# Final stage of an FFT convolution and phase-mixing kernel: the transpose of u by a transposing DMA in place of TensorE

## The chip, the cores and the metric

The kernel runs on one core of one Trainium2 chip. The metric is the device time of one execution, in microseconds (us). Three runs of the kernel before gave 2108.34, 2110.66 and 2111.68 us; the median is 2110.66 us.

## What is computed

Two layers follow one another on `x` of 8 batches x 5696 tokens x 128 channels. The first is a long convolution along the tokens, done by FFT. The second mixes tokens with two 5696 x 5696 matrices, and ends with a small product per token:

```
y  = irfft(rfft(x, 2S) * rfft(h, 2S))[:S]          # first layer, its output is x of the second
theta  = x @ w_theta
zr, zi = x * cos(theta), x * sin(theta)
y  = w_tok_r @ zr + w_tok_i @ zi                    # over tokens, for each batch and channel
u  = x + y
out = u + max(u @ w_ch, 0)                          # the final stage: w_ch is 128 x 128
```

The final stage needs `u @ w_ch`. TensorE sums over partitions, and `u` comes with tokens on partitions, so `u` is transposed to channels on partitions before the product.

## The kernel before

**The order of the stages.** The FFT layer fills about the first 510 us. Then comes the mixing, in two passes over the columns of the token matrices (the sum over source tokens, split in two halves of 2816 tokens, and a remainder of 64). Pass 0 (`p == 0`) sums over the first half and stores partial sums in HBM (`cp_hbm`). Pass 1 (`p == 1`, from about 1285 us) loads those partial sums back, adds the second half and the remainder, and runs the final stage. The change lies in pass 1, save for one moved call in pass 0.

**Pairs and stretches.** Rows of output are worked on in pairs: token tile `tt` and token tile `22 + tt`, each of 128 tokens, and each in two halves of 512 columns (4 batches x 128 channels). So a pair has four output blocks of 128 x 512. The kernel uses Strassen's scheme of seven products (M1 to M7) for a pair, in the order M3, M4, M5, M2, M1, M7, M6 (loop index `n` = 0 to 6). The sum over source tokens is cut in four *stretches* (groups of 3, 3, 3 and 2 blocks of 256), so in one stretch the loop at L1079 issues seven *blocks* of 6 matmuls (4 in the last stretch, and one more for the remainder in four of its blocks). Some pairs at the start of a pass (tt 0, and tt 1 in pass 0) use the plain product ("classic", L1034), and the last 64 tokens have stretches of their own (L953).

**What feeds TensorE.** The weights are loaded by GpSimd's DMA queue (L509) into a ring of six buffers, each by four DMAs of 80 or 96 KB. VectorE transposes them (L714, `wt`) and forms the sums that the scheme needs (L723, `out_`); it also adds the finished products to the output blocks (L1091, two additions for most products, in the last stretch of a pair). At the start of pass 1 the z operands `b` come through ScalarE's DMA queue (L639).

**The output blocks.** In pass 1 a block `c` is loaded by SyncE's queue from `cp_hbm` (L828) into one of six buffers, is added to, goes through the final stage, and is stored to `out` by the same queue (L805). The four blocks of a pair are c12, c21, c11, c22; they go through the final stage one after the other, one in each stretch of the *next* pair, and the load of the fourth block of a pair (c22) goes into the buffer of the second block of the pair before (c21), so it waits for that block's store.

**The final stage, `u_stage` (L785).** `first` makes a bf16 copy `ub` of the block on ScalarE (L791), transposes it by four TensorE transposes of 128 x 128 into the PSUM tile `utp` (L794), and copies that to SBUF as `uts` on ScalarE (L796). `uts` is one buffer, `yt_room()`, a piece of the ring tile, so it is free again only when the product of the block before has read it. `second` issues four matmuls with `w_ch` into `v` (L801), `max(v, 0) + c` on VectorE (L803), and the store (L805). Both PSUM tiles use the bank tagged `misc`.

**Where they are called.** `aside(first_of, second_of)` (L940) is called after each block: where `first_of` is true it takes the next `first` from the list `spread`, where `second_of` is true it runs the pending `second`. In the Strassen loop it is `aside(n == 1, n == 4)` (L1108), in the classic one `aside(n == 0, n == 2)` (L1055). In pass 0 the same calls place background steps of the phase computation (`bg_phase`: transposes L742, theta matmuls L396, ScalarE's and VectorE's steps L398 to L432). The last four blocks of the kernel call `first` and `second` themselves at L1094 to L1104, with tags of their own for `utp`, `v` and `uts`.

Of 90 output blocks, 86 go through `spread`: 4 in the stretches of the last 64 tokens at the start of pass 1, 2 (of 64 tokens) in the pair after them, and 80 in the 20 pairs that follow.

The order of instructions is made by a scheduler from the program's order and the dependencies; VectorE's order is written out by hand only up to the first Strassen pair of a pass.

Of the kernel before, what the change touches and what calls it, by code (L numbers as in the profile page):

```python
# [11 lines left out]
BF16 = mybir.dt.bfloat16  # L12
# [10 lines left out]
def kernel(  # L23
# [10 lines left out]
    nc = tc.nc  # L34
    B, S, D = x.shape
    assert D == 128
    P = 128
# [454 lines left out]
    def small(at, n):  # L492
        return ring["all"][:, WB + BT + at:WB + BT + at + n]
# [5 lines left out]
    def yt_room():  # L499
        return small(0, 4 * P).rearrange("p (b n) -> p b n", b=4)  # L500
# [101 lines left out]
    for g, (bp, dh) in enumerate(groups):  # L602
        st = {}
# [59 lines left out]
    def sum_some(n):  # L663

        for o in [o for o in owed if o[1] <= 2 or done["used"] > o[0]][:n]:
            owed.remove(o)
            o[2]()
# [117 lines left out]
    def u_stage(ti, h, c, m):  # L785
        st = {}

        def first(tags=("misc", "misc", None)):
            st["tags"] = tags
            ub = ybp.tile([P, 4, D], BF16, tag="yb", name="ub")  # L790
            nc.scalar.activation(ub[:m].rearrange("p b d -> p (b d)"), c[:m], AF.Copy)  # L791
            utp = mps.tile([P, 4, P], BF16, tag=tags[0], name="utp")
            for b in range(4):
                nc.tensor.transpose(utp[:, b, :m], ub[:m, b, :], ident_bf[:m, :m])  # L794
            st["uts"] = uts = cp.tile([P, 4, P], BF16, tag=tags[2], name="uts") if tags[2] else yt_room()
            nc.scalar.activation(uts[:, :, :m], utp[:, :, :m], AF.Copy)  # L796

        def second():
            v = mps.tile([P, 512], F32, tag=st["tags"][1], name="v")
            for b in range(4):  # L800
                nc.tensor.matmul(v[:m, b * D:(b + 1) * D], st["uts"][:, b, :m], w_ch_sb,  # L801
                                 start=True, stop=True)
            nc.vector.scalar_tensor_tensor(c[:m], v[:m], 0.0, c[:m],  # L803
                                           op0=ALU.max, op1=ALU.add)
            nc.sync.dma_start(  # L805
                bass.AP(tensor=out.tensor, offset=out.offset + ti * P * D + 4 * h * S * D,
                        ap=[[D, m], [S * D, 4], [1, D]]),
                c[:m].rearrange("p (b d) -> p b d", b=4))
        return nothing, first, second

    tags, where_bg = {"n": 0}, {}
# [100 lines left out]
    nxt, second, st = None, None, {}  # L912
    ordered = ExitStack()
    for i, (k, p, tt, j0, s0, nj) in enumerate(stretches):
# [25 lines left out]
        def aside(first_of, second_of):  # L940
            nonlocal second
            if first_of and spread and (p == 1 or (tt > 0 and not end_of_pair)):
                where_bg["tags"] = ("c2", "c3") if j0 + s0 == TJ else ("red", "mag")
                _, first, second = spread.pop(0)
                with tc.issue_after(sides["late"].ins) if p == 0 and tt == 1 else ExitStack():
                    first()
                    if len(spread) > 1:
                        spread[1][0]()
            if second_of and second is not None:
                second()  # L950
                second = None

        if tt is None:  # L953
# [7 lines left out]
            for j in range(nj):  # L961
                jj = j0 + s0 + j
                for r in range(2):
                    b = [x[:, r, :] for x in bts[jj]]
# [37 lines left out]
        def product(a, jj, j, n, hs):  # L1002
            for r in range(2):
                for h in hs:
                    nc.tensor.matmul(ms[n // 2 * 2 + h], a[n][:, j, :, r],  # L1005
                                     bts_of[p][jj][n % 2 * 2 + h][:, r, :],
                                     start=(n % 2 == 0 and jj == 0 and r == 0), stop=False)
# [26 lines left out]
        if classic:  # L1034
            for n in range(4):
                for j in range(nj):
                    product(a, j0 + s0 + j, j, n, range(2))
                    if p == 0 and (n * nj + j) % 4 != 3:
                        sum_some(1)
                if end_of_pair and n % 2:  # L1040
                    (c12, z12), (c21, z21), (c11, z11), (c22, z22) = cs
                    out_of = (((c11, z11, 0), (c12, z12, 1)), ((c21, z21, 2), (c22, z22, 3)))[n // 2]
                    for h, (c, z, m_) in enumerate(out_of):
                        if p:
                            nc.tensor.matmul(ms[m_], wl[n // 2], zl[h], start=False, stop=True)
                            nc.vector.tensor_tensor(c, z, ms[m_], op=add)
                            continue
                        if n == 1:
                            nc.tensor.matmul(ms[m_], ident_bf, z, start=False, stop=True)
                        else:  # L1050
                            for b in range(4):
                                nc.tensor.matmul(ms[m_][:, b * D:(b + 1) * D], z[:, b, :], ident_bf,
                                                 start=False, stop=(b == 3))
                        nc.scalar.activation(c, ms[m_], AF.Copy)
                aside(n == 0, n == 2)  # L1055
            if end_of_pair and woven:
                for n_ in range(7):
                    step(n_)
            for j in range(nj):
                if p == 0:  # L1060
                    done["used"] = tt * (j0 + s0 + nj)
                else:
                    for op in sum_ops(bts[j0 + s0 + j])[:2]:
                        op()
        else:
            left = {}
            if zl is not None and end_of_pair:
                left = {M5: (wl[0], zl[1]), M7: (wl[0], zl[2]),
                        M2: (wl[1], zl[0]), M6: (wl[1], zl[2])}
            if end_of_pair:  # L1070
                (c12, z12), (c21, z21), (c11, z11), (c22, z22) = cs
                sums = {M3: ((c12, z12, add), (c22, z22, add)), M4: ((c11, z11, add), (c21, z21, add)),
                        M5: ((c11, c11, ALU.subtract), (c12, c12, add)),
                        M2: ((c21, c21, add), (c22, c22, ALU.subtract)),
                        M1: ((c11, c11, add), (c22, c22, add)),
                        M7: ((c11, c11, add),), M6: ((c22, c22, add),)}
            while owed and owed[0][0] < j0 + s0 + nj:
                sum_some(1)
            for n, q in enumerate(ORDER):  # L1079
                sum_some(1)  # L1080
                for j in range(nj):
                    jj = j0 + s0 + j
                    for r in range(2):
                        nc.tensor.matmul(ms[q], a[q][:, j, :, r], bts[jj][q][:, r, :],  # L1084
                                         start=(jj == 0 and r == 0),
                                         stop=(jj == NJ - 1 and r == 1 and q not in left))
                if q in left:
                    nc.tensor.matmul(ms[q], left[q][0], left[q][1], start=False, stop=True)  # L1088
                if end_of_pair:
                    for c, z, op in (sums[q][::-1] if i + 1 == len(stretches) and q == M5 else sums[q]):  # L1090
                        nc.vector.tensor_tensor(c, z, ms[q], op=op)  # L1091
                    if i + 1 == len(stretches):
                        if n == 4:
                            ends = [u_stage(t, h, c, P) for (t, h), (c, _) in zip(where, cs)]  # L1094
                            ends[0][1]((f"m{M3}", f"m{M5}", "yy0"))
                        elif n == 5:
                            ends[1][1]((f"m{M4}", f"m{M2}", "yy1"))
                        elif n == 6:
                            ends[0][2]()
                            ends[2][1]((f"m{M1}", f"m{M3}", "yy2"))  # L1100
                            ends[1][2]()
                            ends[3][1]((f"m{M7}", f"m{M5}", "yy3"))
                            ends[2][2]()
                            ends[3][2]()  # L1104
                    if woven:
                        for n_ in {1: (0, 1), 2: (2,), 3: (3,), 4: (4,), 5: (5,), 6: (6,)}.get(n, ()):
                            step(n_)
                aside(n == 1, n == 4)  # L1108
        if not end_of_pair:
            continue  # L1110
        if i + 1 == len(stretches):
# [35 lines left out]
```

## Time and profile before

| | |
|---|---|
| median of three runs | 2110.66 us (2108.34 to 2111.68) |
| the profiled execution, first to last instruction | span 2116.2 us |
| TensorE busy | 2008.1 us, 95% of the span |
| VectorE busy | 1598.3 us, 76% |
| ScalarE busy | 673.9 us, 32% |
| utp transposes, L794 | x360, busy 34.6 us |
| `uts` copies of the 86 blocks, L796 | x86, busy 50.9 us |
| `ub` copies, L791 | x90, busy 56.3 us |
| v matmuls of the 86 blocks, L801 | x344, busy 33.5 us |
| DMA, all queues | 334.97 MB, 408265 packets |

The profile is one execution. Of it only the span is given, no separate total; it is 5.5 us (0.26%) longer than the median of the timed runs. Engines are PE (TensorE's matmuls), PEld (its weight loads), DVE (VectorE), ACT (ScalarE), POOL (GpSimd) and SP (SyncE); a q behind a name is the engine's queue, which issues DMAs and waits. Matmuls overlap: a group of short ones ends later than the next one starts, so what they take of TensorE is read from the distance between starts. L794 stands for line 794 of the kernel. "A wt<-ring" after an engine means that the instruction writes `wt` and reads `ring`.

### The profile page before, as it was taken

The numbers are of one execution on the slowest core, as the hardware profiler recorded it, in microseconds if no ns is written. First come the engines' busy times: TensorE is split into PE (matmuls) and PEld (weight loads), VectorE is DVE, ScalarE is ACT, GpSimd is POOL, SyncE is SP. The second block draws the span as 40 slices with busy tenths as digits, with TensorE's granted clock in tenths as the row PEclk, the third lists the DMA queues.
The fourth block names the chain that finished last, engine by engine and source line by source line (L and its number), as shares of the span: only waits on it lengthen the run. The fifth ranks groups of instructions, "written<-read, shape, count | busy, mean of one in ns | idle before, by whom it ended". The sixth has DMA issues, their size and how long they took to land.

```text
span 2116.2 us, 41712 instructions
## 1 busy us (share of the span) xinstructions
PE 2008.1 (95%) x15873; PEld 1117.7 (53%) x15873; DVE 1598.3 (76%) x2884; ACT 673.9 (32%) x997; POOL 907.6 (43%) x1662
## 2 busy tenths in 40 slices
PE   4888999778999999999999999999999999999998
PEld 3788888654444444444444444444444444444444
DVE  7767776777778888888886755877777777776867
ACT  5778877774332333332310000111111111111111
POOL 5301010227444536354556543445454444545450
PEclk8799999999999999999999999999999999999999
DMA  6457474889989989898999879878888787979693
GB/s 140 98 130 170 117 180 127 216 245 243 178 153 179 176 176 168 170 176 173 174 165 156 142 137 296 128 117 147 140 143 145 134 153 128 156 127 157 124 156 90
DMA packets 408265, 334.97 MB, mean 158 GB/s; under 512 B 85927, under 2 KB 358439, under 8 KB 407079
## 3 DMA queue, kind: packets, MB, share of 16 engines
q0 software_dynamic: 225952, 156.72, 52.5%
q1 hardware_dynamic: 176128, 164.05, 27.3%
q10 hardware_dynamic: 5984, 11.54, 1.6%
q8 instruction: 124, 2.03, 0.4%
q14 instruction: 77, 0.63, 0.1%
HBM read 377.11 MB, written 92.49 MB: 222 GB/s over the span
## 4 chain that ended last, share of the span: by engine, by line
PE 68%; DMA 3%; DVE 3%; POOL 1%; issue 1%; ACT 0%; DVEq 0%; SPq 0%; POOLq 0%; ACTq 0%
PE m L1084 61%; PE m L1005 2%; DMA ring<-in_moe_w_tok_r_dram 1%; DMA b<-z_hbm 1%; POOL ring L509 1%; PE v L801 1%; PE utp L794 1%; DVE c L1091 1%; PE m L1088 1%; DVE b L655 1%; DVE wt L714 1%; DMA ring<-in_moe_w_tok_i_dram 0%; PE theta_ps L396 0%; PE tpz L742 0%; PE m L968 0%
## 5 line engine op out<-in xcount | busy, mean ns | idle before, releaser
L509 POOL DMA_DIRECT2D ring<-in_moe_w_tok_i_dram x720 | 387.9, 546 | 666.7 <-DVE wt L714 587.7
L714 DVE STREAM_TRANSPOSE wt<-ring 128x384 f32<-128x384 f32 (+2 forms) x720 | 360.5, 527 | 123.2 <-PE m L1084 71.3
L509 POOL DMA_DIRECT2D ring<-in_moe_w_tok_r_dram x720 | 386.4, 546 | 149.3 <-DVE wt L714 86.4
L1084 PE MATMUL m<-b,wt 128*128 128x512 bf16 x1640 | 388.3, 379 | 2.0 <-DVE wt L714 1.7
L1084 PEld LDWEIGHTS <-wt 128*128 128x128 bf16 x1804 | 175.8, 98 | 217.6 <-DVE wt L714 6.2
L1091 DVE TENSOR_TENSOR c<-c,m 128x512 f32<-128x512 f32 x412 | 266.9, 674 | 0.4 <-PE m L1084 0.4
L796 ACT ACTIVATE ring<-utp 128x512 bf16<-128x512 bf16 (+1 forms) x86 | 50.9, 592 | 586.2 <-PE utp L794 586.2
L328 PE MATMUL ps<-r_u,u_t 128*128 128x128 f16 x1024 | 128.6, 226 | 10.8 <-ACT red L419 5.6
L329 PE MATMUL ps<-r_v,v_t 128*128 128x128 f16 x1024 | 127.7, 226 | 0.4
L791 ACT ACTIVATE ub<-c 128x512 bf16<-128x512 f32 (+1 forms) x90 | 56.3, 628 | 215.0 <-DMA ring<-in_moe_w_tok_r_dram 123.8
L1005 PE MATMUL m<-b,wt 128*128 128x512 bf16 x480 | 112.9, 385 | 9.1 <-DVE wt L714 4.4
L130 POOL DMA_DIRECT2D x<-in_x_dram x64 | 33.9, 536 | 189.3 <-PE ps L194 177.8
L328 PEld LDWEIGHTS <-u_t 128*128 128x128 f16 x1024 | 104.1, 102 | 9.6 <-DVE u_t L312 6.2
L329 PEld LDWEIGHTS <-v_t 128*128 128x128 f16 x1024 | 103.4, 101 | 5.7 <-issue 3.2
L310 ACT ACTIVATE xs<-ps 128x1024 f16<-128x1024 f32 x96 | 95.9, 1023 | 15.1 <-DVE v_t L312 7.9
L312 DVE TENSOR_TENSOR u_t<-xs,hs 128x1024 f16<-128x1024 f16 x96 | 68.8, 716 | 32.1 <-ACT xs L310 19.7
L1005 PEld LDWEIGHTS <-wt 128*128 128x128 bf16 x528 | 50.8, 99 | 70.8 <-issue 8.7
L194 PE MATMUL ps<-f_t,x 89*128 89x180 f16 x512 | 77.2, 299 | 5.6 <-ACT xs L310 3.9
L212 PEld LDWEIGHTS <-w_t 64*128 64x128 f16 x3240 | 61.2, 102 | 34.8 <-issue 21.7
L398 ACT ACTIVATE red<-theta_ps,magic 128x512 f32<-128x512 f32 (+1 forms) x46 | 31.6, 687 | 133.7 <-PE theta_ps L396 116.0
L194 PEld LDWEIGHTS <-x 89*128 89x128 f16 x512 | 70.3, 241 | 6.6 <-issue 5.9
L744 ACT ACTIVATE ring<-tpz 128x512 bf16<-128x512 bf16 (+1 forms) x46 | 27.5, 597 | 132.6 <-PE tpz L742 108.9
(2914 smaller groups left out, 3916.7 us busy)
## 6 DMA issues: line engine op xcount, KB each, us to landing
ring<-in_moe_w_tok_r_dram POOLq DMA_DIRECT2D x352, 96.0 KB, 4.4
ring<-in_moe_w_tok_i_dram POOLq DMA_DIRECT2D x352, 96.0 KB, 5.0
ring<-in_moe_w_tok_r_dram POOLq DMA_DIRECT2D x352, 80.0 KB, 4.5
ring<-in_moe_w_tok_i_dram POOLq DMA_DIRECT2D x352, 80.0 KB, 3.9
hs<-hf_hbm SPq DMA_DIRECT2D x192, 128.0 KB, 3.2
cp_hbm<-c SPq DMA_DIRECT2D x88, 256.0 KB, 2.6
c<-cp_hbm SPq DMA_DIRECT2D x88, 256.0 KB, 4.4
out_dram<-c SPq DMA_DIRECT2D x88, 256.0 KB, 4.5
```

The source lines that it names most:

```text
L194: nc.tensor.matmul(ps[:, i // 2, (i % 2) * 2 * K1:(i % 2 + 1) * 2 * K1], lhs(q + i), f1_t[:NB], start=True, stop=True)
L212: nc.tensor.matmul(ps[:, e, j * HD:(j + 1) * HD], w_t2[rows, c0 + j, N2 * (1 - ri):N2 * (3 - ri)], a_st["a"][rows, ri * K1 + c0 + j, :], s ...
L310: nc.scalar.activation(xs[:, :, :, :ck], ps, AF.Copy)
L312: nc.vector.tensor_tensor(uv[r][:, :, :, c0:c0 + ck], xs[:, :, :, :ck], hv[:, r:r + 1, :, :ck].to_broadcast([P, 2, HD, ck]), op=mult)
L328: nc.tensor.matmul(o, u_t[:, at:at + P], r_u, start=True, stop=False)
L329: nc.tensor.matmul(o, v_t[:, at:at + P], r_v, start=False, stop=True)
L509: nc.gpsimd.dma_start(wb[32 * i:32 * i + 32, :ng, :nj * 64], bass.AP(tensor=a.tensor, offset=a.offset + row0 * S + p * H + i * QR + j0 * 6 ...
L714: nc.vector.transpose(wt.rearrange("p j t r -> p (j t r)").bitcast(F32).rearrange("p (j g t) -> p g j t", j=TJ, g=4)[:, :ng, :nj], wb[:, : ...
L791: nc.scalar.activation(ub[:m].rearrange("p b d -> p (b d)"), c[:m], AF.Copy)
L1005: nc.tensor.matmul(ms[n // 2 * 2 + h], a[n][:, j, :, r], bts_of[p][jj][n % 2 * 2 + h][:, r, :], start=(n % 2 == 0 and jj == 0 and r == 0), ...
L1084: nc.tensor.matmul(ms[q], a[q][:, j, :, r], bts[jj][q][:, r, :], start=(jj == 0 and r == 0), stop=(jj == NJ - 1 and r == 1 and q not in left))
L1091: nc.vector.tensor_tensor(c, z, ms[q], op=op)
```

## The change

`first` of `u_stage` gets a second way: when its third tag is None, as it is for the 86 blocks that go through `spread`, the transpose of `ub` is one transposing DMA from SBUF to SBUF, issued by ScalarE's queue, that writes `uts` directly. The four TensorE transposes and ScalarE's copy out of PSUM are left to the last four blocks. The DMA is called transposing DMA, or T, below. The places where `second` is called move: in the Strassen loop from after block n = 4 to after n = 6 in pass 1 (pass 0 keeps 4), in the classic loop from after n = 2 to after n = 3 in both passes.

```diff
@@ u_stage, first
             ub = ybp.tile([P, 4, D], BF16, tag="yb", name="ub")
             nc.scalar.activation(ub[:m].rearrange("p b d -> p (b d)"), c[:m], AF.Copy)
+            if tags[2] is None:
+                st["uts"] = uts = yt_room()
+                nc.scalar.dma_start_transpose(uts[:, :, :m], ub[:m].rearrange("p b d -> p (b d)"))
+                return
             utp = mps.tile([P, 4, P], BF16, tag=tags[0], name="utp")
             for b in range(4):
                 nc.tensor.transpose(utp[:, b, :m], ub[:m, b, :], ident_bf[:m, :m])
-            st["uts"] = uts = cp.tile([P, 4, P], BF16, tag=tags[2], name="uts") if tags[2] else yt_room()
+            st["uts"] = uts = cp.tile([P, 4, P], BF16, tag=tags[2], name="uts")
             nc.scalar.activation(uts[:, :, :m], utp[:, :, :m], AF.Copy)
@@ classic loop
-                aside(n == 0, n == 2)
+                aside(n == 0, n == 3)
@@ Strassen loop
-                aside(n == 1, n == 4)
+                aside(n == 1, n == (6 if p else 4))
```

## The prediction

> **What bounds the kernel now.** I read the chain that ended last first, as shares by engine: TensorE carries 68%. Then the busy times by stage, cut at the start of the steady part of pass 1 and at its end.
>
> ```profile
> PE 68%; DMA 3%; DVE 3%; POOL 1%; issue 1%; ACT 0%; DVEq 0%; SPq 0%; POOLq 0%; ACTq 0%
> ...
> core 0: us, PE busy (x) PEld busy (x) DVE busy (x) ACT busy (x) POOL busy (x), PEclk, DMA share, GB/s
> ...
> 1376.20:2094.10 717.90, 717.90 (x3793) 342.84 (x3791) 534.20 (x1039) 95.11 (x159) 336.07 (x627) 1.00 0.80 139
> ```
>
> From 1376 to 2094 us TensorE is busy in every microsecond, at full granted clock (1.00); VectorE is busy for 74%, ScalarE for 13%. So what is taken off TensorE here shortens the run until something else ends later. How much a transpose takes of TensorE is read from the chain inside one pair (start, us, what; a pair lasts 35.89 us):
>
> ```profile
> 1612.17 5.18 PE m L1084 x24
> 1617.35 0.22 PE utp L794 x4
> 1617.58 3.88 PE m L1084 x18
> 1621.46 0.22 PE v L801 x4
> ```
>
> The chain holds nothing but matmuls, 0.216 us each (5.18/24). Four transposes take 0.22 us, not the 0.38 us that a group's mean would make of the busy time (34.6/360 x 4): they overlap with their neighbours. Last, the DMA side, by stretches of one pair, and the landing times that bear on the new wait:
>
> ```profile
> 1600.00:1605.00 5.00, 5.00 (x28) 2.37 (x26) 5.00 (x11) 1.80 (x3) 0.00 (x0) 1.00 0.18 58
> 1605.00:1612.00 7.00, 7.00 (x40) 3.30 (x38) 7.00 (x14) 1.74 (x3) 0.91 (x2) 1.00 0.24 62
> 1612.00:1636.00 24.00, 24.00 (x130) 11.47 (x127) 14.91 (x31) 1.36 (x3) 16.29 (x31) 1.00 1.11 182
> 1636.00:1641.00 5.00, 5.00 (x28) 2.40 (x27) 5.00 (x11) 1.69 (x3) 0.00 (x0) 1.00 0.24 59
> ...
> b<-z_hbm ACTq DMA_DIRECT2D x20, 512.0 KB, 14.9
> yT<-yt_hbm SPq DMA_DIRECT2D x44, 128.0 KB, 5.0
> wl<-wl_hbm SPq DMA_DIRECT2D x22, 32.0 KB, 1.8
> ...
> c<-cp_hbm SPq DMA_DIRECT2D x1, 256.0 KB, 5.3
> ```
>
> The mean DMA share of 0.80 hides a rhythm: 24 us of each pair with the engines full (1.11, since packets of several queues overlap), 12 us around the pair's end nearly empty. There VectorE is the full one (5.00 of 5.00, 7.00 of 7.00), with the additions of L1091. The columns of the last four lines are KB and us from issue to landing; the last is the load of one output block in the full part.
>
> **The change part by part.**
>
> *Removed.* 344 transposes of 86 blocks. In the 20 steady pairs 80 x 0.216 = 17.3 us of TensorE's chain; the two blocks of 64 tokens 0.4 us; the four in the last 64 tokens' stretches about 0.3 us each (utp at 1326.82, the next matmul at 1327.14), which I take as spent on the wait below. Sum: 17.7 us. ScalarE's 86 copies (50.9 us) go too, worth nothing: ScalarE has 0% of the chain.
>
> *Added: the landing of T.* In the built program T waits for `ub` and for the v matmuls of the block before (one `uts` buffer); v now stands at the end of its stretch and waits for T. So T has from one v to the next: a stretch less v. For stretches of 3 that is 7 x 6 x 0.216 = 9.07 us; for the stretch of 2, which runs from 1633.62 to 1640.98, it is 7.36 less utp and v (0.43), 6.9 us. No T is in the trace. From below, the nearest row is 32 KB of 256-byte pieces, 1.8 us; from above, 512 KB on ScalarE's own queue, 14.9 us, with others of its kind behind it. I take 5.0 to 5.3 us: `yT` has T's size and shape (128 partitions x 4 x 256 bytes) in a stage with a DMA share of 0.95, and a `c` block of twice the size takes 5.3 in the full part. With two hops of 0.1 (utp's end at 1617.58 to the copy's start at 1617.67) T's wait is L = 5.5 us: hidden under 6.9 and 9.07. What it costs without that cover is 20 x [max(0, L - 6.9) + 3 max(0, L - 9.07)]; the gain of 17.3 is gone at L = 7.8; at L = 15.1 (14.9 and the hops) it costs 526 us. In the last 64 tokens' stretches v-to-v is 4.6 to 6.7 us, so one T of four may stall 0.9 us; that takes the gain there. Queued behind a waiting T on ScalarE are only `ub` copies of later blocks, which have a stretch to spare.
>
> The Trainium skill speaks against the change here: "VectorE: DVE Perf Modes", section "The three transpose paths", gives 1309 ns for a 128 x 128 bf16 transpose by DMA against 390 on TensorE, and tells to use TensorE where a PSUM destination will do. The trace has 0.054 us per transpose on TensorE's chain, far below the page's 390. An estimate from that page: four at 1309 in a row are 5.2 us, which changes nothing if it is the whole landing, but if it came on top of 5.5 it would make L = 10.7 and cost about 174 us.
>
> *Added: T's share of the engines.* SyncE's queue moved 176128 packets in 27.3% of 16 engines' span, 52 ns each; 512 pieces of 256 bytes at that price are 1.7 us of all 16 engines. From below, 128 KB at the full part's rate (182/1.11 GB/s) is 0.8; from above, ScalarE's queue (5984 packets in 1.6%) 90 ns each, 2.9. Two and a half T's per pair fall in the full 24 us and stretch it by 4.3 us (2 to 7.3) into the 12 nearly empty ones. Late then are the weight loads. The tightest already stops VectorE for 0.18 us before L714 at 1619.65; the sum made from it at 1620.20 is used by TensorE only at 1626.92, over 6 us later, and VectorE has 9 free us in that part. Cost 0; without the cover, 20 us for each microsecond per pair.
>
> *Moved: v, L803 and the store by two blocks (2.6 us).* Behind the store of c21 on SyncE's queue stands the load of c22, into the same buffer. Store at 1622.68, load at 1627.82, landed 5.3 later at 1633.1; used by the second addition at 1635.4 (the first starts at 1634.79). After: store 2.9 later (L803 now stands behind one more L723), load landed at 1622.68 + 2.9 + 5.1 + 5.3 = 1636.0; and L803 of c11 now stands in VectorE's order just before the additions, so these start 0.65 later, the second at 1636.05. No slack is left there. But the first TensorE work behind is the M2 sum (L723 at 1641.86, done at 1642.41, weights read at 1644.87): 2.46 less 0.65, and less 0.2 for the utp that TensorE no longer runs in that pair, leaves 1.6 us. Cost 0; each microsecond beyond costs 20 us. GpSimd's order is the same as before.
>
> *Moved: the classic loop's `second`.* In pass 0 it touches three phase steps of pair tt 1: theta goes 12 matmuls (2.6 us) later, 2.6 us before the next transposes need the same `misc` bank; ScalarE's two reads take 0.69 + 0.59 us. Cost 0, at most 1.3 us each, 4 in all. VectorE's order differs by two L655 there.
>
> *The end.* The last v of `spread` now follows two of the last four blocks' v; TensorE idles there (0.66 us before utp at 2109.58), and L803 fits before the last two, which start at 2111.23. Five stores instead of four come in the last 5 us: 0 to 0.7 us, I take 0.2.
>
> Sum: 2116.2 - 17.7 + 0.2 = 2098.7 on the profiled execution's span, a ratio of 0.9917; on the median of 2110.66 that is 2093.2.
>
> **The rivals.**
>
> *T eats the gain (L from 7 to 8).* The stretch of 2 is too short and the rest holds. At L = 7.6 it costs 20 x 0.7 = 14 us: 2107. For: DMA is full until 1636, and T of that stretch starts at 1633.4. Against: it is nearly empty from 1636 to 1641.
>
> *T is slower than a stretch: the slower side.* Place: v's weight load on TensorE at the end of each stretch; it decides from L = 7.8. At L = 8.7, 20 x 1.8 = 36: 2129; at L = 10, 20 x (3.1 + 2.8) = 118: 2211. For: nothing in the trace transposes in a DMA, and 128 x 128 x 4 elements may cost far more than a plain copy; other queues keep the engines full. Against: no row that I read in the steady part has a median landing above 5.6 us.
>
> *c22 comes late.* If T delays store and load by 3 us together, 1.4 us per pair reach TensorE: 28 us, 2121. For: the slack computed above is 1.6 us. Against: the later load falls in the emptier part, where such loads took 2.5 to 3.0 us.
>
> That the change does not do what it says is excluded: the built program has 688 fewer instructions on TensorE (344 transposes and their weight loads).
>
> **How the numbers follow.** The forecast, T hidden, has 0.54; T eating the gain 0.12 (0.04 of it still faster, 0.08 within the bound); c22 late 0.06 (0.05 slower, 0.01 same); T slower than a stretch 0.28. About 0.2% (4 us) is what a measurement of this kernel can tell from no change. Faster 0.58, within 0.09, slower 0.33. The forecast's own range is 2089 (1 us each for the moved step, the early and the last blocks, and 1.5 of run to run) to 2100 (the moved step's 4, the end's 0.7, 2 of weight loads). The range has to reach into the slow rival: up to L = 9.4, 20 x (2.5 + 1.0) = 70, so 2165; above lie 0.15, below 0.03.
>
> **What would show it.** Right: TensorE still without gaps in the steady part, a pair of 35.03 us instead of 35.89, no L794 before the last blocks, L801 waiting for nothing, T landing within 6.7 us, the full DMA part longer by 2 to 7 us. Wrong: idle time of PE or PEld before L801 released by the DMA of `uts` (T too slow); before L1084 released by VectorE while L1091 waits for `c` (c22); L714 waiting for weight loads by several us per pair (shared engines).

## The result, and the profile after

| | before | after |
|---|---|---|
| median of the timed runs on one chip | 2109.5 us (2107.35 to 2111.68, 4 runs) | 2145.53 us (2141.16 to 2152.18, 4 runs) |
| span of the profiled execution | 2116.2 us | 2143.4 us |
| the first 19 of the 20 steady pairs | 682.0 us, 35.89 each | 709.8 us, 37.36 each, single ones 34.99 to 40.89 |

The ratio of the times is 1.0161, with a 95% interval of 1.0143 to 1.0179. The change makes the kernel slower by 1.6%. The profiled executions differ by 27.2 us, and the 19 pairs by 27.8: the loss lies in the steady part.

The shares of the chain that ended last, by engine, in the kernel after; before, TensorE had 68% of it:

```profile
PE 39%; DMA 15%; DVE 10%; issue 5%; POOL 3%; DVEq 0%; ACT 0%; SPq 0%; ACTq 0%; POOLq 0%
```

DMAs and VectorE have taken over what was TensorE's. Busy times by stage of the kernel after, in the columns of before (PE, PEld, DVE, ACT and POOL busy, granted clock, DMA share, GB/s). The first line is the steady part, the other three one pair that starts at 1603.86:

```profile
1376.00:2120.00 744.00, 699.77 (x3387) 322.31 (x3455) 516.13 (x1034) 50.45 (x80) 333.78 (x618) 1.00 0.95 147
...
1604.00:1612.00 8.00, 7.92 (x37) 3.45 (x36) 8.00 (x17) 2.52 (x4) 0.00 (x0) 1.00 0.11 23
1612.00:1636.00 24.00, 22.19 (x111) 10.29 (x111) 14.54 (x31) 0.00 (x0) 17.01 (x32) 1.00 1.19 173
1636.00:1642.00 6.00, 5.17 (x27) 2.36 (x27) 3.27 (x6) 0.00 (x0) 0.33 (x1) 1.00 1.30 170
```

TensorE idles for 44.2 of 744 us, at a mean clock of 1.00. The full part of the DMA engines, 24 us of a pair before, now runs to the end of the pair (1.30 in its last 6 us), and VectorE, which was busy all the time there, is busy for 3.27 of 6 us: its additions wait. Who made VectorE wait, between 1376 and 2120 us (sum in us, times, longest):

```profile
DVE wt L714 <- PE m L1088: 69.8, 33, 5.0
DVE c L1095 <- DMA c<-cp_hbm: 53.9, 18, 5.2
```

The second line is new: 18 times an addition waited for a block's load. The landing times (KB, median us from issue) of the loads, the stores, and T:

```profile
c<-cp_hbm SPq DMA_DIRECT2D x88, 256.0 KB, 4.9
out_dram<-c SPq DMA_DIRECT2D x88, 256.0 KB, 5.7
ring<-ub ACTq DMA_TRANSPOSE x86, 6.0
```

T lands in 6.0 us in the median (2.4 to 9.3), near the forecast's 5.0 to 5.3; `v` waited for it 7 times, 6.9 us in all, 5.2 of them in the first six blocks. The stores went from 4.5 to 5.7 us in the median. What that does is in the chain of one pair (start, us, what):

```profile
1625.42 0.60 DVE c L807
...
1626.05 7.39 DMA out_dram<-c
...
1633.50 5.20 DMA c<-cp_hbm
...
1638.73 0.06 DVE c L1095
...
1639.33 0.68 DVE c L1095
```

This is c21's store, the load of c22 into the same buffer, and the addition that needs c22. In the timeline of the kernel before, the same three are, in the pair that starts at 1605.08:

```profile
1622.68 0.39 SPq L805 DMA_DIRECT2D out_dram<-c  x1
1627.82 0.32 SPq L828 DMA_DIRECT2D c<-cp_hbm  x1
...
1634.79 2.44 DVE L1091 TENSOR_TENSOR c<-c,m 128x512 f32<-128x512 f32 x4
```

There the load goes out 5.14 us after the store, and four additions run without a wait. In the kernel after the store takes 7.39 us, and the timeline has the waits behind it:

```profile
1638.73 1.29 DVE L1095 TENSOR_TENSOR c<-c,m 128x512 f32<-128x512 f32 x2 [3.03 <-DMA c<-cp_hbm]
...
1640.40 1.04 PE L1088 MATMUL m<-b,out__21302 128*128 128x512 bf16 x4 [0.78 <-DVE out__21302 L723]
```

VectorE waits 3.03 us for c22, and TensorE then 0.78 us for the sum (`out__21302`) of the pair's last product, M6, which VectorE forms behind the additions.

There is a second stall in many pairs, 18 to 20 us after their start. The timeline of the kernel after, in the same pair:

```profile
1611.43 1.94 DVE L714 STREAM_TRANSPOSE wt<-ring 128x384 f32<-128x384 f32 x4
1612.29 2.16 POOL L509 DMA_DIRECT2D ring<-in_moe_w_tok_i_dram  x4 [14.10 <-DVE wt L714]
...
1621.74 0.58 DVE L714 STREAM_TRANSPOSE wt<-ring 128x384 f32<-128x384 f32 x1 [4.98 <-PE m L1088]
...
1622.82 1.47 PE L1088 MATMUL m<-b,out__21136 128*128 128x512 bf16 x6 [1.70 <-DVE out__21136 L723]
```

VectorE's transposes of four weight tiles free ring buffers, GpSimd then loads new weights, VectorE transposes them (L714 at 1621.74), and TensorE waits 1.70 us for the sum made from them. The matmul that is named as L714's releaser ended at 1621.12, 0.6 us before L714 starts. The fourth of GpSimd's loads, issued at 1613.89, landed at 1621.57, 0.17 us before it: L714 waited for the load. With the stalls of all 19 pairs sorted by place: at the pair's end 13 stalls of 20.1 us in all (11 of them for M6's sum, two 4.4 us into the next pair), 18 to 20 us into the pair 9 stalls of 15.0 us in all, before `v` 1.8 us. Together they are 36.9 of the 44.9 us by which these pairs exceed those of the kernel with neither transposes nor T, below; the rest lies in shorter gaps, in about 0.17 us of overlap between matmuls that each stall interrupts, and in a lower clock behind one stall.

### The profile page after: what moved, and what is told of

Its sections match the earlier page's. It is cut to its first block, busy times and chain, and to the rows that moved or that the text cites. A ratio compares the mean times of both kernels' runs of the same rounds, so it can differ in the third digit from the quotient of the medians.

```text
span 2143.4 us, 40939 instructions
## 1 busy us (share of the span) xinstructions
PE 1982.3 (92%) x15358; PEld 1096.0 (51%) x15529; DVE 1582.0 (74%) x2884; ACT 626.8 (29%) x911; POOL 912.1 (43%) x1662
## 4 chain that ended last, share of the span: by engine, by line
PE 39%; DMA 15%; DVE 10%; issue 5%; POOL 3%; DVEq 0%; ACT 0%; SPq 0%; ACTq 0%; POOLq 0%
PE m L1088 36%; DMA out_dram<-c 5%; DMA ring<-in_moe_w_tok_r_dram 4%; DVE c L1095 4%; POOL ring L509 3%; DMA ring<-in_moe_w_tok_i_dram 2%; DVE wt L714 2%; DMA c<-cp_hbm 2%; DMA ring<-ub 1%; DVE c L807 1%; DVE b L655 0%; PE theta_ps L396 0%; PE m L972 0%; PE m L974 0%; PE tpz L742 0%
## 5 line engine op out<-in xcount | busy, mean ns | idle before, releaser
L714 DVE STREAM_TRANSPOSE wt<-ring 128x384 f32<-128x384 f32 (+2 forms) x720 | 355.6, 520 | 154.6 <-PE m L1088 83.1
L1095 DVE TENSOR_TENSOR c<-c,m 128x512 f32<-128x512 f32 x412 | 267.0, 671 | 54.0 <-DMA c<-cp_hbm 53.9
L312 DVE TENSOR_TENSOR v_t<-xs,hs 128x1024 f16<-128x1024 f16 x96 | 67.7, 706 | 0.0
```

Source lines behind the costliest of these rows:

```text
L312: nc.vector.tensor_tensor(uv[r][:, :, :, c0:c0 + ck], xs[:, :, :, :ck], hv[:, r:r + 1, :, :ck].to_broadcast([P, 2, HD, ck]), op=mult)
L714: nc.vector.transpose(wt.rearrange("p j t r -> p (j t r)").bitcast(F32).rearrange("p (j g t) -> p g j t", j=TJ, g=4)[:, :ng, :nj], wb[:, : ...
```

## The experiments

Each experiment ran beside the kernel before on its chip (medians of before 2111.29, 2112.83, 2110.8 and 2113.54 us for the four groups), so the ratios are what is compared. Below, the *end stall* is the one behind c22's load, the *weight stall* the one 18 to 20 us into a pair.

### The parts of the change

**The moved calls alone** (TensorE's transposes stay):

```diff
-                aside(n == 0, n == 2)
+                aside(n == 0, n == 3)
...
-                aside(n == 1, n == 4)
+                aside(n == 1, n == (6 if p else 4))
```

> TensorE's transposes stay, only second moves (Strassen loop of pass 1 to n = 6, classic loop to n = 3). Theory A (the store of c21 is late by two blocks and then slowed by T, so c22's load comes late, VectorE's additions wait at the pair's end, and through VectorE both TensorE's next blocks and the ring's buffers are late): without T the store takes 5.1 us as before, the slack of 1.6 us holds: additions wait under 1 us per pair, no stall of TensorE, 2106 to 2114 us. Theory A' (the move alone is enough): TensorE stalls 1 to 3 us per pair as in the changed kernel, 2130 us or more. Theory B (T's share of the DMA engines delays the weight loads): 2106 to 2114.

Measured: 2114.38 us, ratio 1.0008 (0.9995 to 1.002). Every steady pair lasts 35.90 us, TensorE is busy in all of 1376 to 2094 us, and no addition waits for c22. The move costs nothing by itself.

**T, with `second` back in its old places:**

```diff
-                aside(n == 0, n == 3)
+                aside(n == 0, n == 2)
...
-                aside(n == 1, n == (6 if p else 4))
+                aside(n == 1, n == 4)
```

> T stays, second goes back to n = 4 and n = 2. Theory A and A': the store of c21 starts at 17.6 us into the pair again; even if it takes 8 us and the load 5.3, c22 lands at 30.9, 0.6 late and within the slack of 2.4: no stall at the pair's end nor 18 us into the pair, about 2093 us. Theory B: the weight loads are late as before, 1 to 2 us per pair remain at 18 us into the pair, 2110 to 2125. Theory C (T's own landing is what TensorE waits for): T now has the shorter way in the first stretch of a pair, the waits before L801 grow above the 17 us of the changed kernel, 2110 or more.

Measured: 2101.24 us, ratio 0.9953 (0.9938 to 0.9968): faster than both kernels, though 8 us above the 2093 expected (where these lie comes under what was not expected). The 19 pairs take 667.0 us, nearly all 35.00. c21's store is slow here too, 6.7 us in the median, but it is issued 17.5 us into the pair and not 21.7, and the additions wait for c22 only 5 times (6.9 us).

**Neither transposes nor T:**

```diff
                 st["uts"] = uts = yt_room()
-                nc.scalar.dma_start_transpose(uts[:, :, :m], ub[:m].rearrange("p b d -> p (b d)"))
                 return
```

> The changed kernel with the transposing DMA left out: uts is not written, so the product uses what stands in that buffer, and nothing is transposed for the 86 blocks; second stays at n = 6. Theory A: the store of c21 takes 5.1 us again, c22 within the slack, 2091 to 2098 us. Theory A': additions wait and TensorE stalls as in the changed kernel, 2125 us or more. Theory B: 2091 to 2098. Tells how much of the loss needs T at all.

Measured: 2091.04 us, ratio 0.9907 (0.9889 to 0.9926), pairs of 35.00 us throughout. This is what taking the transposes off TensorE is worth, 0.93%, if the transpose in their place costs nothing.

**`second` at n = 4 in c21's stretch only, at n = 6 elsewhere:**

```diff
-                aside(n == 1, n == (6 if p else 4))
+                aside(n == 1, n == (6 if p and j0 + s0 != TJ else 4))
```

> The changed kernel, with second back at n = 4 in the one stretch where c21 is finished (the second of a pair), n = 6 in the other three. Theory A and A': c22's load follows that store, so its lateness goes, and with it both stalls: 2093 to 2100 us. Theory B: T's stay where they were, 1 to 2 us per pair at 18 us into the pair remain, 2110 to 2125.

Measured: 2119.54 us, ratio 1.0032 (1.0018 to 1.0047). With c21's store earlier the waits for c22 fall from 53.9 to 5.1 us; but T of c21 has two blocks less between c12's `v` and its own, and `v` waits for it 13 times, 10.7 us. The time lies in theory B's range, but its sign is missing: there is no weight stall. The waits for c22 are thus the larger part of the loss, and T is slow enough to be late where its stretch is cut by 2.6 us.

### What it is in T

The experiments of this part turn on one time in each pair, from the issue of c21's store to that of c22's load, which waits for it. Read from the timeline of each kernel, over 19 pairs:

| | T ahead of c21's store | median us (range) | end stalls | weight stalls |
|---|---|---|---|---|
| before | no | 5.1 (4.0 to 6.0) | 0 | 0 |
| moved calls alone | no | 3.9 (2.5 to 5.9) | 0 | 0 |
| no T | no | 4.7 (3.2 to 6.5) | 0 | 0 |
| T but for c11 | no | 5.3 (3.5 to 7.3) | 0.4 us | 2.1 us |
| T on SyncE's queue, behind the store | behind | 3.6 (2.3 to 4.7) | 0 | 0 |
| T for c11 alone | yes | 7.3 (4.1 to 8.9) | 4.4 us | 0 |
| T for c11 and c22 | yes | 6.6 (4.5 to 8.9) | 10.7 us | 0 |
| a plain DMA in T's place | yes | 7.5 (4.4 to 8.3) | 8.4 us | 0.2 us |
| c21 before c12 | yes | 7.6 (4.8 to 9.9) | 6.9 us | 14.5 us |
| after | yes | 7.9 (5.3 to 9.5) | 20.1 us | 15.0 us |

(With c21 before c12 it is c12's store and c11's load.) In the kernels that are not in the table it is 6.7 with `second` back at n = 4 and 6.5 with it there for c21 only, both with T ahead, and 4.6 in the last candidate, with T behind the store. So wherever a DMA is issued right ahead of that store, it takes 6.5 to 7.9 us, and elsewhere 3.6 to 5.3. The sums of stalls are those of one profiled execution each: that of "T but for c11" took 7 us less than the median of its kernel, that of "T for c11 and c22" 11 us more.

**T for c11 left out, and T for c11 alone.** T of c11 is issued at c21's `v`, in the kernel after 0.9 to 2.9 us before c21's store, 1.5 in the median.

```diff
+                if not (ti < 22 and h == 0):
-                nc.scalar.dma_start_transpose(
+                    nc.scalar.dma_start_transpose(
```

> The changed kernel with the transposing DMA left out for c11 alone, the one that is issued with the store of c21; the other three of a pair stay (uts of c11 is not written, output not the reference's). Theory A, the loss comes from that one neighbour of the store: pairs of 35.0 to 35.3 us, no waits of the additions for c22, time 2092 to 2102. Rival B, the transposing DMAs burden the engines as a whole: three quarters of the 54 us between the changed kernel and the one without any stay, 2131.

Measured: 2107.08 us (2096.57 to 2115.17), ratio 0.9965 (0.9944 to 0.9986); the profiled execution has a span of 2098.0. The median is 5 us above theory A's range and 24 below rival B's 2131. Its one weight stall comes in the pair behind the one with the end stall.

```diff
+                if ti < 22 and h == 0:
-                nc.scalar.dma_start_transpose(
+                    nc.scalar.dma_start_transpose(
```

> The changed kernel with the transposing DMA for c11 alone, left out for the other three blocks (their uts is not written, output not the reference's). Theory A, that one DMA makes c22 late: nearly the whole loss, 2128 to 2146, pairs of 36.7 to 37.4 us. Rival B, burden as a whole: a quarter of the 54 us, 2104.

Measured: 2102.42 us, ratio 0.9944 (0.9925 to 0.9963). Theory A's size was wrong: this T alone doesn't make the whole loss, and the time is near rival B's 2104. But rival B's shares don't hold either, since the other three T's should then have cost three times as much, 2131. Theory A's place was right. The timeline of this kernel, at T and c21's store:

```profile
1474.20 1.21 ACTq L795 DMA_TRANSPOSE ring<-ub  x1
...
1475.49 0.39 SPq L810 DMA_DIRECT2D out_dram<-c  x1
...
1483.34 0.32 SPq L833 DMA_DIRECT2D c<-cp_hbm  x1
...
1487.16 1.29 DVE L1096 TENSOR_TENSOR c<-c,m 128x512 f32<-128x512 f32 x2 [1.86 <-DMA c<-cp_hbm]
```

The load goes out 7.85 us after the store that it waits for, the addition waits 1.86 us, and this pair lasts 35.25 us. Over its pairs a wait of 2.29 gives 35.46 us, 2.89 gives 36.06, 3.74 gives 36.71: beyond 1.6 to 2.1 us each microsecond of waiting costs one. There is no weight stall at all.

So the loss isn't the sum of its parts: against none, the three T's cost 12 us and the one 8 us (ratios 0.9965 and 0.9944 less 0.9907, times 2111), all four 54 us. The weight stall needs both: the late c22, and T's of c12 and c21 beside the weight loads. Where there is only the first, as in the pair of this kernel that starts at 1455.13, GpSimd's loads start 8.65 us into the pair and the transpose of the weights comes 7.34 us later, in time. Where there is neither, the timeline of the kernel without T has, in the pair that starts at 1485.82:

```profile
1492.36 2.27 POOL L509 DMA_DIRECT2D ring<-in_moe_w_tok_i_dram  x4 [12.96 <-DVE wt L714]
...
1499.22 0.58 DVE L714 STREAM_TRANSPOSE wt<-ring 128x384 f32<-128x384 f32 x1 [2.38 <-PE m L1087]
```

That is 6.54 us into the pair and 6.86 us more. In the kernel after, in the lines shown above, it is 8.43 us into the pair and 9.45 us more: 1.9 us from the late start, 2.6 us from slower loads, and 1.70 us of them reach TensorE. The other pairs say the same. In the kernel after, the nine pairs with a weight stall are those in which GpSimd's loads start 8.1 us or later and the first four take 8.7 us or more to land; in the other ten these take 7.7 at most. With T for c11 alone the loads start at 8.4 us or later in twelve pairs, but the first four land in 5.9 to 7.4 us.

**T for c11 and c22 only** tests that:

```diff
+                if (ti < 22) == (h == 0):
-                nc.scalar.dma_start_transpose(
+                    nc.scalar.dma_start_transpose(
```

> The changed kernel with the transposing DMA for c11 and c22 only (left out for c12 and c21, whose uts is not written; output not the reference's). c11 alone cost 11 us over none, the other three 16, all four 54. Theory A, two tolerances that meet: the late c22 makes VectorE's and so GpSimd's weight loads of the next pair start late, and TensorE waits for the weight tile some 19 us into a pair only if the transposing DMAs of c12 and c21 then slow these loads: without them that second stall is absent, and the time is that of c11 alone or little more, 2102 to 2110. Rival B, the cost grows with the number of transposing DMAs: half of 54, 2118 or more, with stalls 19 us into the pair.

Measured: 2109.2 us (2099.27 to 2120.28), ratio 0.9984 (0.996 to 1.0007). No weight stall in any pair, as theory A has it (the first four loads land in 6.6 us or less), and 16 us over none (0.9984 less 0.9907), less than half of 54. The time lies in theory A's range, but not near c11 alone: some of these stalls cost more than their length, for a reason that comes under what was not expected.

**A plain DMA in T's place**, the same bytes in the same 512 pieces, on the same queue:

```diff
-                nc.scalar.dma_start_transpose(uts[:, :, :m], ub[:m].rearrange("p b d -> p (b d)"))
+                nc.scalar.dma_start(uts[:m], ub[:m, 0:1, :].to_broadcast([m, 4, D]))
```

> The changed kernel with the transposing DMA replaced by a plain DMA from SBUF to SBUF on the same queue at the same place, with the same bytes written in the same 512 pieces of 256 bytes (it copies the first of the four blocks four times, so the output is not the reference's). Theory A, transposing itself is what slows the store of c21 beside it: the store lands in 4 to 5 us as without any DMA there, the additions wait for c22 hardly at all, pairs of 35.0 us, time 2091 to 2099. Rival B, any 128 KB on ScalarE's queue ahead of that store does it: pairs near 37.4 us, store landing 7 to 9 us, time 2138 to 2148.

Measured: 2112.03 us, ratio 0.9993 (0.9981 to 1.0005), between both theories. The store of c21 is as late as with T and the additions wait 45.8 us for c22, nearly as much as with T; so any 128 KB ahead of that store make it late. But less of that reaches TensorE. The ScalarE queue's packets take less here: 4.1% of 16 engines' span against 5.4% with T and 1.6% without either, that is 0.61 us of all 16 engines for a plain copy and 0.95 for T. That difference in the engines' time is the likely reason that the loss is 18 us over none (0.9993 less 0.9907) and not 54; no run shows it by itself.

**The order of T and store.** The DMA view cut in slots of 2 us from the issue of c21's store (packets, MB, share of 16 engines; q0 is GpSimd's queue, q1 SyncE's, q10 ScalarE's). First the kernel without T, its second slot, 2 to 4 us behind the store's issue:

```profile
q0 software_dynamic: 385, 0.26, 87.5%
q1 hardware_dynamic: 415, 0.22, 36.6%
```

Then the kernel after, the same slot:

```profile
q0 software_dynamic: 231, 0.16, 98.2%
q10 hardware_dynamic: 532, 0.13, 54.2%
q1 hardware_dynamic: 9, 0.01, 1.7%
```

In the first slot, in both kernels, SyncE's queue ends the load issued before the store (134 and 130 packets). In the second it moves the store where there is no T; in the kernel after T's 532 packets go by and 9 of SyncE's, and the store follows in the third and fourth (325 and 200). T takes 1.08 us of all 16 engines there, and SyncE's queue all but stands still for 2 us. The pair shown is a clear one. Over the 19 pairs of the kernel after, the 15 slots up to 6 us behind the store's issue in which 350 or more of T's packets went by had 0 to 189 of SyncE's, 25 in the median; the second slot of the kernel without T had 102 to 513, 424 in the median.

**T on SyncE's queue, behind the store** that goes out at the same `v`:

```diff
-                nc.scalar.dma_start_transpose(uts[:, :, :m], ub[:m].rearrange("p b d -> p (b d)"))
+                with tc.issue_after(after[0].ins) if after[0] else ExitStack():
+                    nc.sync.dma_start_transpose(uts[:, :, :m], ub[:m].rearrange("p b d -> p (b d)"))
...
-            nc.sync.dma_start(
+            after[0] = nc.sync.dma_start(
...
-            if first_of and spread and (p == 1 or (tt > 0 and not end_of_pair)):
+            if first_of and spread and not (p and second) and (p == 1 or (tt > 0 and not end_of_pair)):
...
                 second = None
+                if p and tt is not None and spread:
+                    _, first, second = spread.pop(0)
+                    first()
```

> The changed kernel with each transposing DMA issued by SyncE's queue, directly behind the store that goes out at the same v, instead of by ScalarE's queue ahead of it. Theory A, the store is late because the transposing DMA is ahead of it: the store of c21 lands in 4 to 5 us again and the additions no longer wait for c22; the transposing DMA now lands later itself, some 7.5 to 8 us behind v, which fits a stretch of 3 and is up to 1.2 us late in the stretch of 2: 2091 to 2115. Rival B, it slows the store by being in flight beside it, in whichever order: the waits for c22 stay, 2125 to 2150.

Measured: 2152.56 us, ratio 1.0197 (1.0158 to 1.0237). The time lies above both ranges, and the waits show why. Who waited in 1376 to 2120 us, first VectorE's, then TensorE's largest:

```profile
DVE wt L714 <- PE m L1094: 59.3, 39, 3.0
```

```profile
PE v L808 <- DMA ring<-ub: 36.5, 20, 3.0
```

No addition waits for c22, and there is neither end stall nor weight stall: with the store first the chain of the loss is gone, though as many T's run. (T and the store are also on one queue here and not on two; whether T would slow a store that went out before it on another queue was not tried.) In its place `v` of c12 waits in 18 of the 19 pairs: T of c12 now stands on SyncE's queue behind c22's store, which goes out only 5.7 us into the pair.

**c21 before c12 in the final stage**, so that the load behind the late store is c11's:

```diff
-        finish(p, tt, 1, c12)
-        finish(p, 22 + tt, 0, c21)
+        for f in ((22 + tt, 0, c21), (tt, 1, c12))[::1 if p else -1]:
+            finish(p, *f)
```

> The changed kernel with c21 before c12 in the order in which a pair's blocks go through the final stage. Then c22's load waits for a store of the first stretch, and the load that waits for the late store is c11's, which the additions need 0.65 to 0.87 us later than c22. Theory A, the loss is that late load: the waits for c fall by 0.65 to 0.87 us in each of the 18 pairs that have one, the stalls behind them with them: 2115 to 2132. Rival B, the transposing DMAs burden the weight loads whatever the order of the blocks: 2140 to 2150.

Measured: 2129.35 us, ratio 1.0095 (1.0058 to 1.0132), 14 us less than the change. The additions still wait in 18 pairs, 36.8 us for 53.9, that is 0.95 less each where 0.65 to 0.87 was expected; seven of these waits the view puts down to TensorE, though c11's load landed 0.08 to 0.12 us before they ended. The end stalls fall by 13.2 us, and the weight stalls stay (14.5 for 15.0 us): the time is in theory A's range, but only the end stalls follow it.

### Candidates

**T with `second` after n = 4, and TensorE for the first six blocks** (against the second experiment):

```diff
+    u_seen, EARLY = [], 6
...
-            if tags[2] is None:
+            if tags[2] is None and len(u_seen) >= EARLY:
...
+            u_seen.append(1)
             utp = mps.tile([P, 4, P], BF16, tag=tags[0], name="utp")
...
-            st["uts"] = uts = cp.tile([P, 4, P], BF16, tag=tags[2], name="uts")
+            st["uts"] = uts = cp.tile([P, 4, P], BF16, tag=tags[2], name="uts") if tags[2] else yt_room()
```

> A candidate: the transposing DMA with the second half back after n = 4 (2101.2 us in its run), and the first six blocks (the last 64 tokens' stretches and the pair behind) transposed by TensorE as before. In that run v waited 1.16 + 1.14 + 1.76 us for the DMA in those six, and six groups of transposes cost about 6 x 0.25 = 1.5: 2101.2 - 4.1 + 1.5 = 2098.6. Rival, those waits lie under loads that end last in that part anyway: 2101 to 2103.

Measured: 2101.52 us, ratio 0.9942 (0.9922 to 0.9963). That overlaps the 0.9953 without this edit, so a gain from those six blocks is not shown; the time is in the rival's range.

**T of c12 by ScalarE, the others by SyncE behind the store, TensorE for the first six:** the two edits above, and

```diff
+                on_act = ti < 22 and h == 1
-                with tc.issue_after(after[0].ins) if after[0] else ExitStack():
-                    nc.sync.dma_start_transpose(
+                with tc.issue_after(after[0].ins) if after[0] and not on_act else ExitStack():
+                    (nc.scalar if on_act else nc.sync).dma_start_transpose(
```

> A candidate and a test of the last wait: v stays after n = 6; the transposing DMA of c12 is issued by ScalarE's queue as in the changed kernel (its store neighbour goes out 5.7 us into the pair, when that DMA has landed), those of c21, c11 and c22 by SyncE's queue directly behind the store; the first six blocks are transposed by TensorE. With all on SyncE the only wait left in the steady pairs was v's for the DMA of c12, 0.8 to 3.0 us some 11 us into the pair, since that one stood behind c22's store. Theory A: that wait goes, no waits for c22 appear, pairs of 35.0 to 35.3 us, 2092 to 2103, at or below the 2101 of the kernels with v after n = 4. Rival B, transposing DMAs beside weight loads cost TensorE something whatever the order: pairs above 36 us, 2112 or more.

Measured: 2122.04 us (2106.38 to 2126.9), ratio 1.0031 (1.0011 to 1.0051). Neither theory: the time is in rival B's range, but there is no end or weight stall, and the waits for c22 are 8.8 us and reach nobody. What costs is T's own landing: behind the store it lands in 6.6 us from its issue in the median, and `v` waits for it 17 times, 21.9 us. With `second` after n = 6 one of the two is late: T if the store goes first, the store if T does.

## Why the prediction was wrong

It forecast 2093.2 us, faster; the kernel is slower, at 2145.5. Its steps one by one:

- *What bounds the kernel, and "Removed"*: right. Without transposes and T the ratio is 0.9907, or 19.6 us (15.6 to 23.4), where 17.7 was worked out, and a pair is 35.00 us for 35.03. Undisturbed pairs of the changed kernel reach 34.99 us.
- *"Added: the landing of T"*: right for the steady part. 5.0 to 5.3 us was taken, 6.0 measured, and `v` waits 1.8 us in the 19 pairs; in the first six blocks it waits 5.2 us, where 0.9 was allowed. Four transposes land in 2.4 us in the nearly empty part. The estimate drawn from the Trainium skill ("VectorE: DVE Perf Modes", "The three transpose paths"), 5.2 us of transposing on top of a plain landing, is not seen (the page's advice to prefer TensorE stands in its next section, "Rules for kernel authors"): the plain DMA in T's place lands in 5.3 us in the median, T in 6.0. The rival "T is slower than a stretch", the largest on the slow side, was not what happened.
- *"Added: T's share of the engines"*: the size held, 1.08 us in one slot and 0.95 in the mean, for 1.7 (0.8 to 2.9). The step asked only whether weight loads had cover, in a pair where VectorE is on time. They have; they lose it when VectorE is late.
- ***"Moved: v, L803 and the store by two blocks"*: the step that failed.** It took 5.1 us for the store's landing, from a row without T, and 1.6 us of tolerance behind it. The size of the tolerance held (1.6 to 2.1 us in the kernel with T for c11 alone), though the first TensorE work behind the additions is not the next pair's M2 sum, as the step has it, but M6's sum in the same pair. The finding that no slack is left before it held too. But the move and T come together: T is issued at the same `v` that releases the store, is out before it, and its packets go first. From the store's issue to the load's it takes 7.9 us in the median for the 5.1 assumed. The later issue was sized rightly: 3.0 us in the median of the pairs without a weight stall, for 2.9. The move alone costs nothing, and T alone at n = 4 about 10 us over none (0.9953 less 0.9907); their meeting at one `v` was put at nothing, and the two together cost 54.
- *The rival "c22 comes late"*, with 0.06, names this mechanism and its place. It gave 28 us, 2121. The end stalls of the 19 pairs are 20.1 us; the weight stalls, 15.0 us more, stand in neither this rival nor the sum. They come when an addition that waited leaves VectorE late into the next pair, so that GpSimd's loads start 1.9 us late and then run beside T's.
- *Moved classic `second`*: within the ratio 1.0008 of the moves alone, no cost. *The end* was not tried by itself.

The margin was visible beforehand: a chain of store, load and addition with 1.6 us to spare, and a DMA newly put ahead of its first link.

## What to carry to other kernels

Work that is taken off the bounding engine and given to a DMA can be paid for by the DMAs issued just behind it: before such a change, look for the transfer that is released by the same event and follow what waits for it, to its last microsecond of slack. Put the new DMA, or that transfer, in another place (here `second` two blocks earlier turns 1.6% slower into 0.5% faster). And cost parts of a change that meet at one instruction together: here the move alone cost nothing and T alone about 10 us, and the two together 54.

## What was not expected

**A queue all but stands still while another's short packets pass.** In the slot shown SyncE's queue moved 9 packets in 2 us while T's 532 went by, and all queues together 150 GB/s, against 238 in the same slot without T. With the plain DMA in T's place, SyncE's moved 2 to 229 in such slots, 95 in the median, against 25 with T. Why the engines don't mix these two queues, as they do mix either with GpSimd's, was not settled.

**Behind some stalls of TensorE its clock is lower.** In the kernel with T for c11 and c22, after a stall of 3.27 us, one window (columns as before, the granted clock is the third number from the end):

```profile
1640.40:1646.00 5.60, 5.55 (x21) 2.30 (x22) 5.60 (x11) 1.26 (x2) 0.00 (x0) 0.70 0.23 60
```

Four matmuls take 1.91 us instead of 1.03 there, and the pair that starts in it lasts 36.75 us without a stall of its own. Within it the granted clock was 0.50 for 3.4 us (1641.80 to 1645.20). The same followed stalls of 2.43, 2.22 and 2.75 us in that kernel and of 2.93 us in the kernel after, but not one of 2.62 us there, nor one of 3.09 us with `second` at n = 4 for c21 only. With T on SyncE's queue it came with five of the 18 waits of `v` for c12's T. The five pairs that it falls in are 1.6 to 1.9 us longer than their stalls account for, 8.9 of the 12 us by which the pairs there exceed 19 x 35.0 and the waits for T. Why it follows some stalls and not others was not settled.

**About 8 us of the 0.9% stay unused in the best version.** With T after n = 4 the steady pairs are as short as without T, but the first of them starts at 1388.70 us for 1380.83. Waits of `v` for T account for 1.16 + 1.14 + 1.76 us of that, and 1.8 us are there before anything that was changed: the first store of a partial sum in pass 0 goes out at 529.63 us for 527.88. With TensorE for those blocks the first steady pair starts at 1388.92, with that first store at 531.29. So these single executions differ by 1.8 to 3.4 us by themselves, and the cause of the rest stays open.
